# The last sum of a decode kernel: x added by TensorE, the result turned onto 128 partitions and stored as 128 short rows

## The chip, the core and the metric

The kernel runs on one NeuronCore of a Trainium2 chip (trn2). The metric is the device time of one execution in microseconds (us); three executions of the kernel before took 1304.88, 1305.26 and 1305.73 us, median 1305.26. The profile is of one further execution. In it and in the text, PE is the matrix engine (TensorE), PEld its loading of weights, DVE the vector engine, ACT the scalar engine, POOL is GpSimd, and SP the engine that issues most of the transfers. DMA engines, 16 of them, move data between the device memory and SBUF (the on-chip memory of 128 partitions); matmuls write to PSUM, a smaller memory beside PE, likewise of 128 partitions.

## The reference

One token (a vector x of 512 floats) goes through a layer norm, and then through attention over a cache of 65536 keys and an MLP, side by side. The result is the sum of both and of x itself. All is float32.

```python
xn = _layernorm(x, axis=-1)
return x + _A_ref(xn, A_k_cache, A_v_cache, A_wq, A_wo) + _B_ref(xn, B_w1, B_w2)

# _A_ref: 32 query heads, 8 key/value heads of 65536 keys x 128
q = (x @ wq).reshape(...)
scores = einsum("bhqd,bhkd->bhqk", q, k) * (Dh ** -0.5)
o = einsum("bhqk,bhkd->bhqd", softmax(scores), v)
return o.reshape(B, Sq, Hq * Dh) @ wo          # 4096 -> 512

# _B_ref
h = maximum(einsum("bsd,df->bsf", x, w1), 0)   # 512 -> 1792
return einsum("bsf,fd->bsd", h, w2)            # 1792 -> 512
```

The caches are 2 x 268 MB, the weights some 24 MB; everything is read once.

## The kernel before, in words

The kernel is written with one queue of instructions for each engine and explicit semaphores. A small class, Flow (lines 43 to 65), counts an engine's instructions: `op` issues one, after waiting for the marks that it is given, and `mark` is the engine's count so far. The helper `load` (line 150) issues one DMA and makes a semaphore for it; all loads and the one store go through its line 152, so in the profile they stand under L152 (the loads of k and v in the loop stand under L175, L297 and L299).

The work goes in four stages.

1. Start. x is loaded twice on ACT's queue: as 128 rows of 4 floats (tile xT, for the layer norm) and as 4 rows of 512 bytes at partitions 0, 32, 64 and 96 of the tile x4 (line 202; x4 is cleared before by DVE). wq is loaded on SP's queue, and q is made.
2. The loop over 8 heads x 4 parts of the cache (32 steps). SP loads 8 MB of k and 8 MB of v for each step as soon as the buffers ks and vs are free. PE makes scores (L329), DVE turns them by 32x32 blocks (L361, a stream transpose from PSUM), ACT takes the exponential (L407), PE multiplies with v (L345), DVE accumulates (L387).
3. The MLP's first half. w1 and w2 go into ks and wo into vs, when these are free. wo is cut into 32 slices of 128 x 512 floats and loaded by six DMAs of 16, 8, 4, 2, 1 and 1 slices (line 38), so that the last to land is small.
4. The end, lines 423 to 521. PE multiplies with w1 (L428), DVE takes the maximum with 0 (L435) and turns it (L269), PE and DVE put the heads' sums together (L439 to L472). Then comes the last product. `gather` (L483) accumulates 14 slices of w2 and the first 24 slices of wo, each of 512 columns with one column of weights; slice j goes to row 32 x (j mod 4) of the PSUM tile acc_z. So four matmuls stand side by side in the array, each on its own 32 of the 128 columns, and acc_z holds four partial sums of the same 512 values. DVE copies acc_z to `rows` (L498). Then acc_y takes over: its row 32c, with c from 0 to 3, holds the 128 results 128c to 128c + 127. L501 sums the four partial sums into it with a column of ones, one matmul for each c. The last eight slices of wo (j from 24 to 31) go straight to acc_y, four matmuls a slice, one for each c (L510). DVE adds x (L516), in place in x4, and SP stores 4 rows of 512 bytes (line 518). SP then waits for the store (line 521), and the engines' closing semaphores end the execution.

PE's instructions are carried out in the order in which they are written, and what sets that order at the end is the order of the slices of wo. Between the copy L498 and the store there is no other work for PE, DVE and SP.

The change lies in stage 4. The functions that it touches:

Of the kernel before, what the change touches and what calls it, by code (L numbers as in the profile page):

```python
# [15 lines left out]
P = 128  # L16
# [5 lines left out]
CT = 4  # L22
# [13 lines left out]
SLICES = R * G  # L36
# [32 lines left out]
def attention_and_mlp_kernel(  # L69
# [29 lines left out]
    te, ve, se, ge, sy = nc.tensor, nc.vector, nc.scalar, nc.gpsimd, nc.sync  # L99
# [4 lines left out]
    def place(name, *shape):  # L104
        return sb.tile([P, *shape], F32, name=name)
# [3 lines left out]
    tr = place("tr", NT * SUB, 32)  # L109
    wt = place("wt", NT * SUB, G)  # L110
    xT, xc, sq, xn = (place(n, A) for n in ("xT", "xc", "sq", "xn"))
    x4 = place("x4", P)
    sw = place("sw", SLICES)
    mine = place("mine", HKV)

# [5 lines left out]
    ident, ones = place("ident", P), place("ones", P)  # L121
# [13 lines left out]
    rows = place("rows", 512)  # L135
# [4 lines left out]
    acc_o, acc_z, acc_y, pm = (ps.tile([P, 512], F32, name=n) for n in ("acc_o", "acc_z", "acc_y", "pm"))  # L140

    names = "k_in v_in tiles scores m_out bias_out a_out w_out o_out k_free v_free q_in d_out f_out f_free"
    with tc.tile_critical():
# [4 lines left out]
        PE, DV, AC, GP = (Flow(nc, e, n) for e, n in ((te, "pe"), (ve, "dve"), (se, "act"), (ge, "pool")))  # L148

        def load(engine, name, dst, src, n=16):  # L150
            sem = nc.alloc_semaphore(name)
            engine.dma_start(dst, src).then_inc(sem, n)  # L152
            return sem, n
# [33 lines left out]
        for t in (acc_o, acc_z, pm):  # L187
# [6 lines left out]
                out=ident, in_=ident, pattern=[[-1, P]], base=0, channel_multiplier=1,  # L194
# [5 lines left out]
        x4_in = None  # L200
        se.wait_ge(*x4_free)
        x4_in = load(se, "x4_in", x4[0:P:32, :], x.rearrange("(c n) -> c n", c=CT))
# [72 lines left out]
        for i in range(SLICES):  # L275
            c = i % CT
# [3 lines left out]
                    start=(i < CT), stop=(i >= SLICES - CT),  # L280
# [41 lines left out]
        with nc.Fori(0, STEPS, engines=[ENG.PE]):  # L322
            te.wait_ge(k_in, 16).then_inc(k_in, -16)
            te.wait_ge(q_in, 1).then_inc(q_in, -1)  # L324
            for s in range(NT):
                pt = (pa, pb)[s // 2 % 2][:, s % 2, :]
                for c in range(CT):
                    at = (s * CT + c) * TW
                    i = te.matmul(pt[32 * c : 32 * c + 32, :], qcur, ks[:, at : at + TW], start=True, stop=True)  # L329
# [12 lines left out]
            n = NT * SUB // WIDE  # L342
            for i in range(n):
                c = i % CT
# [4 lines left out]
                    start=(i < CT), stop=(i >= n - CT),  # L349
# [5 lines left out]
        with nc.Fori(0, HKV, engines=[ENG.DVE]):  # L355
            for n in range(NP):
                for s in range(0, NT, 2):
                    if s == NT - 2:

                        ve.wait_ge(s_tiles, NT // 2).then_inc(k_free, 1)  # L360
                    i = ve.transpose(  # L361
                        tr[:, s * SUB : (s + 2) * SUB, :].rearrange("p b i -> p (b i)"),
                        (pa, pb)[s // 2 % 2].rearrange("p i k -> p (i k)"),
                    )._wait_ge(s_tiles, s // 2 + 1)
# [5 lines left out]
                i = ve.reduce_max(top, tr[:, :, :G].rearrange("p b g -> p g b"), axis=AX.X)  # L370
                if n:
                    ve.drain()
                    i = ve.tensor_max(m, m, mc)  # L373
# [29 lines left out]
        with nc.Fori(0, HKV, engines=[ENG.Activation]):  # L403
            for n in range(NP):
                se.wait_ge(s_bias, 1).then_inc(s_bias, -1)  # L405
                for g in range(G):
                    i = se.activation(  # L407
                        wt[:, :, g], tr[:, :, g], AF.Exp, bias=bias[:, n, g : g + 1],
                        scale=scale, accum_out=part[:, n, g : g + 1],
                    )  # L410
# [13 lines left out]
        for a in range(A):  # L424
            for c in range(CT):
# [4 lines left out]
                        start=(a == 0), stop=(a == A - 1),  # L430
# [49 lines left out]
        def gather(c, lhsT, row, marks, last=False):  # L480

            PE.op(
                lambda e: e.matmul(acc_z[32 * c : 32 * c + 1, :], lhsT, row, start=c not in begun, stop=last),  # L483
                *marks,
            )
            begun.add(c)

        for j in range(FB):
            gather(j % CT, hT[:, j : j + 1], t2[:, j * D : (j + 1) * D], [hT_in, w2_in])

        for j in range(SLICES):
            row = vs[:, j * D : (j + 1) * D]
            lhsT = sw[:, j : j + 1]
            if j < DIRECT:
                gather(j % CT, lhsT, row, [sw_in, wo_in[j]], last=(j >= DIRECT - CT))
                if j == DIRECT - 1:

                    DV.op(lambda e: e.tensor_copy(rows, acc_z), PE.mark)  # L498
                    for c in range(CT):
                        PE.op(  # L500
                            lambda e: e.matmul(  # L501
                                acc_y[32 * c : 32 * c + 1, :P], ones[:, 0:1], rows[:, c * P : (c + 1) * P],
                                start=True, stop=False,
                            ),
                            DV.mark,
                        )
            else:
                for c in range(CT):
                    PE.op(
                        lambda e: e.matmul(  # L510
                            acc_y[32 * c : 32 * c + 1, :P], lhsT, row[:, c * P : (c + 1) * P],
                            start=False, stop=(j == SLICES - 1),
                        ),
                        sw_in, wo_in[j],
                    )
        DV.op(lambda e: e.tensor_add(x4, acc_y[:, :P], x4), PE.mark, x4_in)  # L516
        sy.wait_ge(*DV.mark)
        done = load(sy, "y_out", out.rearrange("(c n) -> c n", c=CT), x4[0:P:32, :])

    with tc.tile_critical():  # L520
        sy.wait_ge(*done)
# [29 lines left out]
```

## Time and profile before

| | |
|---|---|
| median of three executions | 1305.26 us (1304.88 to 1305.73) |
| the profiled execution's own time | 1305.38 us |
| its span, from first to last instruction | 1303.3 us |
| read from device memory | 560.99 MB, 430 GB/s over the span |
| PE busy | 662.4 us (51%) |
| DVE busy | 268.9 us (21%) |
| ACT busy | 75.9 us (6%) |
| granted PE clock, mean | 0.734 of full |
| granted PE clock, 1293 us to 1302 us | 1.00 |
| last copy of acc_z (L498) | starts at 1296.95 us |
| last matmul (L510) | ends at 1300.08 us |
| add of x (L516) | 1300.10 us, 0.29 us long |
| issue of the store on SP | 1300.42 us, 0.67 us long |

Shares are of the span. A group line of the profile has the line in the kernel, the engine, the operation, output <- inputs, shapes (partitions x elements) and count; then busy us and mean ns of one; then the engine's idle time before it and what ended it. A timeline line has start and length in us first. Starts count from the span's start. A float32 matmul leaves two records, since PE goes over it twice. Matmuls are pipelined: the length of a record has the way through the array in it, so the pace is read from the distance of starts and not from the length of one.

### The profile page before, as it was taken

What the parts mean: (1) busy time and instruction counts of PE and PEld (TensorE: products, weight loads), DVE (VectorE), ACT (ScalarE), POOL (GpSimd) and SP (SyncE); (2) the same over time, 40 slices, a digit from 0 to 9 for tenths busy, and PEclk for the clock granted to TensorE, in tenths of its full rate; (3) what the DMA queues carried; (4) which work ended last, traced back from release to release, by engine and by line L of the source; (5) the groups of instructions that cost most, each with busy time, mean ns of one, the idle gap of its engine ahead of it and who ended that gap; (6) DMA issues with size and microseconds to landing.
All of it is one profiled execution on the core that took longest, in us unless ns stands there. A gap on an engine that the chain in (4) does not pass through costs nothing. (4 is left out here: it accounts for less than half of the span.)

```text
span 1303.3 us, 10616 instructions
## 1 busy us (share of the span) xinstructions
PE 662.4 (51%) x4562; PEld 243.2 (19%) x4562; DVE 268.9 (21%) x395; ACT 75.9 (6%) x292; POOL 5.4 (0%) x22
## 2 busy tenths in 40 slices
PE   4355446445445535445545535544544644553657
PEld 2121112112112112111211111221111212111123
DVE  2221122221122222012222112222112222211222
ACT  0000000000000000000000000000000000000000
POOL 0000000000000000000000000000000000000000
PEclk9677687777677677677778677767767666767768
DMA  9999999999999999999999999999999999999998
GB/s 418 419 445 422 447 422 447 420 447 422 440 428 430 438 422 445 424 445 424 445 422 447 422 447 420 443 426 436 432 426 443 424 443 424 445 424 445 422 429 346
DMA packets 10821, 561.06 MB, mean 430 GB/s; under 512 B 1336, under 2 KB 1344, under 8 KB 1728
## 3 DMA queue, kind: packets, MB, share of 16 engines
q1 hardware_dynamic: 10664, 560.99, 99.5%
q8 instruction: 3, 0.05, 0.0%
q10 hardware_dynamic: 152, 0.00, 0.0%
q14 instruction: 2, 0.02, 0.0%
HBM read 560.99 MB, written 0.00 MB: 430 GB/s over the span
## 5 line engine op out<-in xcount | busy, mean ns | idle before, releaser
L345 PE MATMUL acc_o<-vs,wt 128*16 128x512 f32 x2048 | 292.0, 734 | 180.1 <-PEq L341 180.1
L329 PE MATMUL pa<-ks,qcur 128*32 128x512 f32 x1024 | 183.6, 814 | 328.9 <-PEq L324 328.9
L361 DVE STREAM_TRANSPOSE tr<-pa 128x1024 f32<-128x1024 f32 x64 | 80.0, 1250 | 421.4 <-PE pa L329 421.4
L329 PE MATMUL pb<-ks,qcur 128*32 128x512 f32 x1024 | 144.0, 653 | 0.0
L329 PEld LDWEIGHTS pa<-ks,qcur 128*32 128x32 f32 x1024 | 64.3, 133 | 416.2 <-issue 403.7
L345 PEld LDWEIGHTS acc_o<-vs,wt 128*16 128x16 f32 x2048 | 68.9, 113 | 376.4 <-issue 376.4
L407 ACT ACTIVATE wt<-tr,bias 128x128 f32<-128x128 f32 x128 | 64.3, 511 | 1085.3 <-ACTq L405 1085.3
L387 DVE SCALAR_TENSOR_TENSOR acc<-acc,alpha,acc_o 128x512 f32<-128x512 f32 x24 | 17.9, 747 | 352.5 <-PE acc_o L345 352.5
L361 DVE STREAM_TRANSPOSE tr<-pb 128x1024 f32<-128x1024 f32 x64 | 80.0, 1250 | 45.5 <-PE pb L329 45.5
L329 PEld LDWEIGHTS pb<-ks,qcur 128*32 128x32 f32 x1024 | 66.2, 129 | 78.3 <-issue 58.4
L334 PE MATMUL pm<-ident,m 128*4 128x128 f32 x32 | 10.0, 313 | 87.0 <-DVE m L373 66.6
L385 DVE COPY acc<-acc_o 128x512 f32<-128x512 f32 x8 | 5.5, 692 | 118.9 <-PE acc_o L345 118.9
L335 PE MATMUL pm<-dg,ones 4*128 4x4 f32 x64 | 15.0, 302 | 21.4 <-DVE dg L377 21.4
L370 DVE TENSOR_REDUCE mc<-tr 128x4 f32<-128x512 f32 x24 | 24.1, 1006 | 1.8
L334 PEld LDWEIGHTS pm<-ident,m 128*4 128x4 f32 x32 | 2.6, 81 | 116.0 <-DVE m L373 88.4
L407 ACT ACTIVATION_READ_ACCUMULATOR wt<-tr,bias 128x1 f32 x128 | 23.9, 187 | 0.0
L335 PEld LDWEIGHTS pm<-dg,ones 4*128 4x128 f32 x64 | 12.2, 236 | 28.8 <-DVE dg L377 28.8
L336 PE MATMUL pm<-dg,rowg 4*128 4x1 f32 x64 | 14.3, 290 | 0.0
L336 PEld LDWEIGHTS pm<-dg,rowg 4*128 4x128 f32 x64 | 13.0, 249 | 0.0
L278 PE MATMUL pa<-vs,tr 128*8 128x512 f32 x64 | 9.9, 769 | 6.1 <-DMA vs<-wq 4.8
L375 DVE TENSOR_REDUCE mg<-pm 4x1 f32<-4x128 f32 x32 | 8.9, 279 | 13.0 <-PE pm L334 13.0
L378 DVE COPY bias<-pm 128x5 f32<-128x5 f32 x32 | 5.2, 163 | 27.8 <-PE pm L336 27.8
(90 smaller groups left out, 116.6 us busy)
## 6 DMA issues: line engine op xcount, KB each, us to landing
vs<-wq SPq DMA_DIRECT2D x1, 7168.0 KB, 21.4
ks<-w SPq DMA_DIRECT2D x2, 3584.0 KB, 22.1
vs<-wo SPq DMA_DIRECT2D x1, 4096.0 KB, 16.4
vs<-wo SPq DMA_DIRECT2D x1, 2048.0 KB, 20.9
vs<-wq SPq DMA_DIRECT2D x1, 1024.0 KB, 4.9
vs<-wo SPq DMA_DIRECT2D x1, 1024.0 KB, 22.9
ks<-k SPq DMA_DIRECT2D x32, 29.2
vs<-v SPq DMA_DIRECT2D x32, 29.3
```

The source lines that it names most:

```text
L278: lambda e: e.matmul(pr[32 * c : 32 * c + HKV, :], xs[:, i, :], vs[:, i * 512 : (i + 1) * 512], start=(i < CT), stop=(i >= SLICES - CT),),
L329: i = te.matmul(pt[32 * c : 32 * c + 32, :], qcur, ks[:, at : at + TW], start=True, stop=True)
L334: te.transpose(pm[:G, :P], m, ident)._wait_ge(s_dve, 3).then_inc(s_max, 1)
L335: te.matmul(pm[:, P : P + G], ones[:G, :], dg[:, :G], start=True, stop=True)._wait_ge(s_dve, 4)
L336: te.matmul(pm[:, P + G : P + G + 1], rowg, dg[:, G : G + 1], start=True, stop=True).then_inc(s_max, 1)
L345: mm = te.matmul(acc_o[32 * c : 32 * c + WIDE * G, :], wt[:, i * WIDE : (i + 1) * WIDE, :].rearrange("p b g -> p (b g)"), vs[:, i * 512 : ...
L361: i = ve.transpose(tr[:, s * SUB : (s + 2) * SUB, :].rearrange("p b i -> p (b i)"), (pa, pb)[s // 2 % 2].rearrange("p i k -> p (i k)"),)._ ...
L370: i = ve.reduce_max(top, tr[:, :, :G].rearrange("p b g -> p g b"), axis=AX.X)
L375: ve.reduce_max(mg, pm[:G, :P], axis=AX.X)._wait_ge(s_max, 1)
L385: ve.tensor_copy(flat, acc_o)
L387: ve.scalar_tensor_tensor(flat, flat, alpha[:, n : n + 1], acc_o, op0=ALU.mult, op1=ALU.add)
L407: i = se.activation(wt[:, :, g], tr[:, :, g], AF.Exp, bias=bias[:, n, g : g + 1], scale=scale, accum_out=part[:, n, g : g + 1],)
```

## The change

Four things are changed, all in stage 4.

- The places in acc_y. Row 32c still holds results 128c to 128c + 127, but result 4i + j of them now lies in column 32j + i. To that end the moving operand of every matmul into acc_y is read in another order: `cut` takes the 128 columns of c, and goes over i (32 values, a step of 4 floats) inside j (4 values, a step of 1 float). `places4` writes them in order.
- x. Four more matmuls, behind those of L501: the row 32c of x4, one partition, with a single one as weight, is added to row 32c of acc_y. The vector engine's add is gone, and the wait on the load of x4 stands on PE now.
- The turn. In place of the add, DVE transposes acc_y by 32x32 blocks into a new tile yt (128 partitions x 32 x 4 floats, 512 bytes a partition). Row 32c of block j becomes column 0 of the transposed block, and the output is written with a step of 4 floats, so that the four floats `yt[p, 0, :]` of partition p are the results 4p to 4p + 3.
- The store. One DMA of 128 rows of 16 bytes from yt, in place of 4 rows of 512 bytes from x4. Both are issued by SP through line 152.

```diff
-    x4 = place("x4", P)
+    x4, yt = place("x4", P), place("yt", 32, 4)
...
+        def cut(row, c):
+
+            return row[:, c * P : (c + 1) * P].rearrange("p (i j) -> p j i", j=4)
+
+        def places4(c):
+            return acc_y[32 * c : 32 * c + 1, :P].rearrange("p (j i) -> p j i", j=4)
+
...
                         PE.op(
                             lambda e: e.matmul(
-                                acc_y[32 * c : 32 * c + 1, :P], ones[:, 0:1], rows[:, c * P : (c + 1) * P],
-                                start=True, stop=False,
+                                places4(c), ones[:, 0:1], cut(rows, c), start=True, stop=False,
                             ),
                             DV.mark,
+                        )
+                    for c in range(CT):
+                        own = slice(32 * c, 32 * c + 1)
+                        PE.op(
+                            lambda e: e.matmul(
+                                places4(c), ones[own, 0:1], cut(x4[own], 0), start=False, stop=False,
+                            ),
+                            x4_in,
                         )
             else:
                 for c in range(CT):
                     PE.op(
                         lambda e: e.matmul(
-                            acc_y[32 * c : 32 * c + 1, :P], lhsT, row[:, c * P : (c + 1) * P],
-                            start=False, stop=(j == SLICES - 1),
+                            places4(c), lhsT, cut(row, c), start=False, stop=(j == SLICES - 1),
                         ),
                         sw_in, wo_in[j],
                     )
-        DV.op(lambda e: e.tensor_add(x4, acc_y[:, :P], x4), PE.mark, x4_in)
+
+        DV.op(lambda e: e.transpose(yt.rearrange("p i j -> p j i"), acc_y[:, :P]), PE.mark)
         sy.wait_ge(*DV.mark)
-        done = load(sy, "y_out", out.rearrange("(c n) -> c n", c=CT), x4[0:P:32, :])
+        done = load(sy, "y_out", out.rearrange("(p j) -> p j", j=4), yt[:, 0, :])
```

## The prediction

> **What bounds the kernel now.** I read the page's slices first, then the timeline of the last 35 us, then groups by form, then the issues of the load helper (L152) and the semaphore instructions behind the store.
>
> The page's head, its DMA row (busy tenths of the DMA engines in 40 slices) and its HBM row:
>
> ```profile
> span 1303.3 us, 10616 instructions
> ...
> DMA  9999999999999999999999999999999999999998
> ...
> HBM read 560.99 MB, written 0.00 MB: 430 GB/s over the span
> ```
>
> The DMA engines are full in every slice but the last: the kernel streams 561 MB, and no engine's work in the loops sets the time. The change touches nothing before the last slices, so it can win or lose only in the tail, where DMA has run dry. The timeline of that tail (start us, length us, engine, line, operation, operands, count, idle before it):
>
> ```profile
> 1283.14 3.62 PE L461 MATMUL pb<-oT,tr 128*128 128x32 f32 x16 [0.28 <-DVE oT L458]
> 1286.69 4.52 PE L483 MATMUL acc_z<-ks,hT 128*1 128x512 f32 x26
> ...
> 1296.95 0.69 DVE L498 COPY rows<-acc_z 128x512 f32<-128x512 f32 x1 [9.08 <-PE acc_z L483]
> 1297.69 0.10 PEld L501 LDWEIGHTS acc_y<-rows,ones 128*1 128x1 f32 x8 [1.84 <-DVE rows L498]
> 1297.69 0.40 PE L501 MATMUL acc_y<-rows,ones 128*1 128x128 f32 x8 [0.91 <-DVE rows L498]
> 1297.80 1.52 PEld L510 LDWEIGHTS acc_y<-vs,sw 128*1 128x1 f32 x56
> 1297.91 2.05 PE L510 MATMUL acc_y<-vs,sw 128*1 128x128 f32 x64
> 1299.56 0.10 PEld L510 LDWEIGHTS acc_y<-vs,sw 128*1 128x1 f32 x8 [0.23 <-DMA vs<-wo]
> 1300.10 0.29 DVE L516 TENSOR_TENSOR x<-acc_y,x 128x128 f32<-128x128 f32 x1 [2.46 <-PE acc_y L510]
> 1300.42 0.67 SPq L152 DMA_DIRECT2D y<-x  x1
> ```
>
> From 1296.95 on this is one chain: copy, 4 matmuls of L501, 32 of L510, add, store. Each f32 matmul is two records. Four matmuls, one for each 32-row block of acc_y, run side by side; I call them a group. A group's pitch is 0.22 us (L501 starts at 1297.69, the next group at 1297.91; the loads say the same, 56 records or 7 groups in 1.52). Eight groups of L510 and one of L501 lie here. The last waited for its slice of wo: its natural start is 1297.91 + 7 x 0.218 = 1299.44, its real one 1299.56. So the slack that DMA gives PE is 0.12 us. The last matmul ends at 1300.08.
>
> **The change, part by part.** The sum is made against the profiled execution: 1305.38 us, of which 1303.3 is span and 2.08 lies around it. The runs' median, 1305.26, is 0.12 below it.
>
> *The extra group (x by PE).* Four more matmuls behind L501: one more group, 0.22. Its wait on x4's load hides behind everything (issued at 1.4 us, landed by 10.1). With reads at today's rate, 0.12 of the 0.22 is taken out of the wait for wo: +0.10. Its rows are one partition each, so the array is used in another shape and then goes back. The row for a change of shape is L461 (128 columns of weights) to L483 (one): the last of L461 ends at 1286.76, L483 starts at 1286.69, so nothing is emptied; but L483 starts 0.33 after the last L461 start, against L461's pitch of 0.22, so 0.11 is lost. Bounds for two switches: 0, and 2 x (0.27 duration - 0.11 pitch of one record) = 0.33, if the array empties each time. I take 0.1, near the row. The Trainium skill, TensorEngine Tiling (Array Packing), Key Properties, says that a change of tiling mode drains the engine; the trace at L461 to L483 shows no drain, and by that rule the term would be 0.33 and the sum 0.2 higher.
>
> *The strided reads.* This is the term that decides. All ten groups (L501, x, eight of L510) now read their moving operand with a step of 4 floats, 16 bytes, since cut() puts j outside i. PE reads one element in 0.109/128 = 0.85 ns today (two records per 0.218 us, four streams side by side). No matmul of this trace reads with such a step, so I bound by the vector engine's rows:
>
> ```profile
> L400 DVE TENSOR_REDUCE fin<-masked 128x128 f32<-128x512 f32 x1 | 1.1, 1062 | 0.0
> ...
> L394 DVE TENSOR_TENSOR masked<-acc,selb 128x512 f32<-128x512 f32 x1 | 0.7, 683 | 0.0
> L472 DVE TENSOR_REDUCE sw<-tr 128x32 f32<-128x256 f32 x1 | 0.6, 611 | 0.0
> L465 DVE TENSOR_TENSOR tr<-pb,mine 128x256 f32<-128x256 f32 x1 | 0.4, 425 | 3.7 <-PE pb L461 3.7
> ```
>
> L394 and L465 read in order: (683 - 425)/256 = 1.01 ns an element and 167 ns fixed. L472 reads SBUF with exactly a step of 16 bytes (h inside g), L400 with 512: (611 - 167)/256 = 1.73 and (1062 - 167)/512 = 1.75 ns. So a stepped float costs 1.73 ns there. If PE's reads are held to the same 1.73 ns, a group goes from 0.218 to 0.218 x 1.73/0.85 = 0.44. Lower bound: no cost. Upper bound beside 0.44: PE's four streams share what one has, 4 x 0.218 = 0.87. I take 0.44, the nearest row by step, type and memory. Before: last matmul ends at 1297.69 + 8 x 0.218 + 0.31 tail = 1299.74 for the eighth group, then the DMA wait, 1300.08. After: 1297.69 + 10 x 0.44 + 0.31 = 1302.40, and the wait for wo is long over. Difference +2.3, extra group included; DMA no longer covers any of it.
>
> *The vector instruction.* An add of 128 elements (291 ns) becomes one transpose of 128 x 128 from PSUM. The profile's row for one is L361: 1250 ns for 1024 columns; at 1.04 ns a column that leaves 183 fixed, so 316 ns for 128. It writes with a step of 16 bytes; if writes pay as reads do, 183 + 128 x 1.73 = 404. So +0.03 to +0.11; I take +0.06. Nothing covers it: PE ended before, SP waits behind.
>
> *The store.* The issues of L152 at the start and the end, and what follows on SP (duration min/median/max in ns; start range):
>
> ```profile
> L152 ACTq DMA_DIRECT2D xT<-x x1: 413/413/413, 0.9 to 0.9; - x1
> L152 ACTq DMA_DIRECT2D x<-x x1: 1075/1075/1075, 1.4 to 1.4; - x1
> ...
> L152 SPq DMA_DIRECT2D y<-x x1: 667/667/667, 1300.4 to 1300.4; - x1
> ...
> L143 SPq EVENT_SEMAPHORE  x3: 17/28/28, 1301.5 to 1301.8; - x3
> ```
>
> The two 4-row transfers hold their queue 1.10 us until the next instruction (y: 1300.42 to 1301.52; x4 the same on ACT); a 128-row one holds SP 0.46 (wq, 0.96 to 1.41). So SP is free 0.64 sooner. But SP then waits for the landing: the trace's semaphore record has the store's last increment at 1302.11, 1.69 after the issue, and SP's wait for it ends at 1302.17, just in the cadence of the instructions before it. So the landing starts to bind as soon as SP is earlier. What it becomes: xT, the one load of 128 rows of 16 bytes, moved its first packet 1.05 after issue (y 1.27); the first packets of the 16 engines spread over some 0.25 (wq's queue); eight packets of 7 ns each, some 0.05 to 0.1; from y's semaphore packets to the landing 0.33. Together 1.05 + 0.25 + 0.08 + 0.33 = 1.71 against 1.69: nothing gained or lost. Bounds: -0.3 if the engines start together and the landing follows at once; +2.3 if each engine's eight rows go one after another at 0.33 each (7 x 0.33). I take 0, since xT is the nearest row.
>
> *Sum.* +2.3 (PE) + 0.1 (shape) + 0.06 (DVE) + 0 (store) = +2.46 on 1305.38: 1307.8 by the profiled execution, 1307.7 by the median.
>
> **Rivals.**
> - *PE reads with a step for free* (chance 0.22). For: PE already takes 0.85 ns for a float, and its port is not the vector engine's. Against: 0.85 is still half of 1.73. Then +0.10 + 0.1 + 0.06 = +0.26: 1305.5. The Trainium skill, SBUF — State Buffer, Specifications (TRN2), wants two hits per 16-byte line for full bandwidth; no run here shows that for PE, and by it this case loses to mine.
> - *Faster* (0.07). Reads free, and the store's engines start together, so that the landing comes at 1.39: +0.26 - 0.3 = 0 to -0.3 with a shape change at no cost: 1305.1. The point from which it decides: the landing has to come more than 0.26 us earlier than 1.69. For: SP is released 0.64 sooner. Against: xT landed 4.3 after its issue (beside other loads), not 1.4.
> - *The small rows are slow to land* (0.06): up to +2.3 on top of my sum, half of it as a middle: 1308.9; on free reads 1306.7. For: nothing in this trace writes 16-byte rows. Against: xT's packets took 7 ns each. The Trainium skill, DMA: Bandwidth & Descriptors, Specifications, says that under 512 bytes the engine reads, modifies and writes; no run here shows it.
> - *The four streams share one read rate* (0.05): ten groups of 0.87, +6.7: 1312.0. Against: today four streams keep the pitch that one stream's records have.
>
> **How the numbers follow.** My case has 0.60. Its own range is 1306.9 (1.45 ns an element, no cost for the shape) to 1308.5 (shape 0.33, DVE 0.11, a store later by 0.3). Over all cases 1305.1 to 1308.5 leaves out about half of the faster case, most of the slow landing and the shared streams, under 0.2 together. 0.2% is 2.6 us, about what a measurement of this kernel can tell from no change: above 1307.87 is slower. My forecast lies just inside, so 0.40 of my case goes over (0.24), with most of the last two rivals: slower 0.33. Below 1302.6 nothing worked out here reaches: faster 0.01. Same 0.66.
>
> **What would show it.** The groups of the last eight slices of wo at a pitch of 0.44 instead of 0.22, with no wait for wo on the last: right; at 0.22: the free reads. The transpose's duration, 316 to 404 ns. The store's issue at some 0.41 instead of 0.67, and the next instruction on SP 0.46 behind its start. The landing 1.7 after the issue. It is wrong if PE's pitch stays, if the gap around the x group is longer than 0.33, or if the store lands later than 2 us after its issue.

## The result and the profile after

| | before | after |
|---|---|---|
| median of the executions (22 of each, side by side) | 1305.32 us (1304.88 to 1305.73) | 1307.32 us (1307.05 to 1308.00) |
| ratio, 95% interval | | 1.0016 (1.0009 to 1.0023) |
| the profiled execution's own time | 1305.38 us | 1307.57 us |
| its span | 1303.3 us | 1305.5 us |

The change makes the kernel slower by 2.0 us, 0.16%: clear of zero, and inside the 0.2% that the prediction took as its bound.

The page after, its head, the DMA row (busy tenths) and the HBM row:

```profile
span 1305.5 us, 10631 instructions
...
DMA  9999999999999999999999999999999999999997
...
HBM read 560.99 MB, written 0.00 MB: 430 GB/s over the span
```

The stream is what it was; the last slice of the DMA row is emptier by a tenth, in line with a tail without transfers that is longer by 2 us. The tail in the timeline of after (start us, length us, engine, line, operation, operands, count, idle before; L508 is now the sum of rows, L516 the group of x, L524 the slices of wo, L530 the turn):

```profile
1296.69 0.69 DVE L505 COPY rows<-acc_z 128x512 f32<-128x512 f32 x1 [11.35 <-PE acc_z L483]
...
1297.43 0.63 PE L508 MATMUL acc_y<-rows,ones 128*1 128x128 f32 x8 [0.89 <-DVE rows L505]
1298.00 0.10 PEld L516 LDWEIGHTS acc_y<-x,ones 1*1 1x1 f32 x8 [0.46 <-issue]
1298.00 0.63 PE L516 MATMUL acc_y<-x,ones 1*1 1x128 f32 x8
1298.55 3.28 PEld L524 LDWEIGHTS acc_y<-vs,sw 128*1 128x1 f32 x64 [0.46 <-issue]
1298.56 3.81 PE L524 MATMUL acc_y<-vs,sw 128*1 128x128 f32 x64
1302.51 0.41 DVE L530 STREAM_TRANSPOSE yt<-acc_y 128x128 f32<-128x128 f32 x1 [5.13 <-PE acc_y L524]
1302.94 0.35 SPq L152 DMA_DIRECT2D y<-yt  x1
```

What the reader is to see: the 64 records of wo take 3.81 us where they took 2.05 with the wait for the last slice in it. No weight load waits for DMA any more (before, the last eight waited 0.23). The groups of L508, L516 and L524 begin at 1297.43, 1298.00 and 1298.56, 0.56 apart, of which 0.45 is a group and the rest a gap.

The store's issue and the semaphore instructions of SP behind it (duration min/median/max in ns; range of starts):

```profile
L152 SPq DMA_DIRECT2D y<-yt x1: 347/347/347, 1302.9 to 1302.9; - x1
```
```profile
L143 SPq EVENT_SEMAPHORE  x3: 17/28/28, 1303.7 to 1304.0; - x3
```

From the issue to SP's next instruction 0.76 us pass (1302.94 to 1303.70), before it was 1.10; from the issue to the end of the span 2.56, before 2.90.

The two profiles add up. From the first matmul into acc_y to the end of the last (as DVE is released), PE takes 5.05 us instead of 2.39: +2.66. The turn takes 408 ns where the add took 291: +0.12. The store gives 0.34 back. The copy of acc_z happens to start 0.26 earlier in the profile of after: -0.26. The sum is +2.18; the spans differ by 2.19.

### The profile page after: what moved, and what is told of

Its sections match the earlier page's. It is cut to its first block, busy times and chain, and to the rows that moved or that the text cites. A ratio compares the mean times of both kernels' runs of the same rounds, so it can differ in the third digit from the quotient of the medians.

```text
span 1305.5 us, 10631 instructions
## 1 busy us (share of the span) xinstructions
PE 673.0 (52%) x4570; PEld 248.1 (19%) x4570; DVE 269.1 (21%) x395; ACT 75.9 (6%) x292; POOL 5.3 (0%) x22
## 5 line engine op out<-in xcount | busy, mean ns | idle before, releaser
L345 PE MATMUL acc_o<-vs,wt 128*16 128x512 f32 x2048 | 295.5, 742 | 176.3 <-PEq L341 176.3
L329 PE MATMUL pb<-ks,qcur 128*32 128x512 f32 x1024 | 147.1, 664 | 0.0
L329 PEld LDWEIGHTS pb<-ks,qcur 128*32 128x32 f32 x1024 | 69.4, 131 | 77.9 <-issue 58.5
```

The lines of the kernel that those rows point to most:

```text
L345: mm = te.matmul(acc_o[32 * c : 32 * c + WIDE * G, :], wt[:, i * WIDE : (i + 1) * WIDE, :].rearrange("p b g -> p (b g)"), vs[:, i * 512 : ...
```

## The experiments

The theory: the reads with a step of 16 bytes double PE's time for every group into acc_y, and all else is small. The main rival: the extra group with its change of shape, or the turn and the store, make the loss. Where a kernel "reads in order", the host lays out the columns of wo and, in the same way, w2 in the order in which acc_y wants them (`order` is that permutation), which needs no arithmetic and no step in the reads; the result stays the same.

Times are medians, of 10 or 11 executions of each kernel and 19 or 26 of the kernel before.

| kernel | time, us | before beside it, us | ratio (95% interval) |
|---|---|---|---|
| stepped reads alone | 1306.78 | 1305.23 | 1.0012 (1.0002 to 1.0022) |
| after, reads in order | 1305.23 | 1305.23 | 1.0000 (0.9991 to 1.0010) |
| x on PE alone | 1305.50 | 1305.22 | 1.0001 (0.9992 to 1.0011) |
| turn and store alone | 1305.16 | 1305.22 | 0.9999 (0.9990 to 1.0009) |
| x early, reads in order | 1305.08 | 1305.22 | 0.9999 (0.9989 to 1.0008) |

The other kernels ran once each; what they are for is read from their profiles, not from their times.

### Stepped reads alone

The kernel before, with the reads of after; DVE's add reads PSUM back in the right order.

```diff
-  acc_y[32 * c : 32 * c + 1, :P], lhsT, row[:, c * P : (c + 1) * P],
+  places4(c), lhsT, cut(row, c),
...
-  DV.op(lambda e: e.tensor_add(x4, acc_y[:, :P], x4), PE.mark, x4_in)
+  x4_out = x4.rearrange("p (i j) -> p i j", j=4)
+  DV.op(lambda e: e.tensor_add(x4_out, acc_y[:, :P].rearrange("p (j i) -> p i j", j=4), x4_out), PE.mark, x4_in)
```

> The kernel before with one thing changed: every matmul into acc_y reads its moving operand with a step of 16 bytes; DVE's add reads PSUM back in the right order, x stays with DVE, the store stays 4 rows. Theory (the stepped reads make the loss): the groups' pitch is 0.45 us instead of 0.22, nine groups end some 1.9 to 2.1 later (9 x 0.235 less the 0.12 of slack to the last slice of wo), time 1307.2 to 1307.4. Rival (the extra group of x with its change of shape, or the turn, makes the loss, and a stepped read only lengthens a matmul's way through the array): pitch 0.22, time 1305.3 to 1305.6.

The timeline of this kernel (as above):

```profile
1297.19 0.63 PE L507 MATMUL acc_y<-rows,ones 128*1 128x128 f32 x8 [0.89 <-DVE rows L504]
1297.40 3.53 PEld L516 LDWEIGHTS acc_y<-vs,sw 128*1 128x1 f32 x64
1297.63 3.83 PE L516 MATMUL acc_y<-vs,sw 128*1 128x128 f32 x64
1301.60 0.29 DVE L524 TENSOR_TENSOR x<-acc_y,x 128x128 f32<-128x128 f32 x1 [4.46 <-PE acc_y L516]
```

Eight groups of loads in 3.53 us: the pitch is 0.44 to 0.45; the trace's starts give 0.227 for each pass over a group where before it is 0.109. PE takes 4.38 us for nine groups; the nine of before take 2.26 without the wait for wo. That is +2.12 for the step alone. The time rises by 1.55, less than I had expected (1.9 to 2.1): the slack to wo is larger than the 0.12 that I read from the profile of before (below). The rival is out as the main cause: nothing of x, the turn or the new store is in this kernel.

One thing more is in this trace. DVE's add reads PSUM here with a step of 32 floats, 128 bytes, and takes 293 ns where it took 291 in order. So not every stepped read costs.

### After, with its reads in order

```diff
+  order = np.arange(D).reshape(CT, 32, 4).transpose(0, 2, 1).reshape(D)
...
-  "wo": np.asarray(A_wo).reshape(HKV, G, DH, D).transpose(0, 2, 1, 3),
+  "wo": np.asarray(A_wo).reshape(HKV, G, DH, D).transpose(0, 2, 1, 3)[..., order],
...
-  places4(c), lhsT, cut(row, c), start=False, stop=(j == SLICES - 1),
+  places4(c), lhsT, row[:, c * P : (c + 1) * P], start=False, stop=(j == SLICES - 1),
```

> The kernel after with its reads put in order: the columns of wo and w2 are laid out on the host in the order in which acc_y wants them, so only the four matmuls of x read with a step. x on PE, the turn and the 128-row store stay. Theory: the groups of rows and of wo go back to a pitch of 0.22, the x group keeps 0.45 and two gaps of 0.12 around it, PE ends 0.3 later than before, the transpose costs 0.12 more than the add, the store gives 0.34 back: time within 0.3 of before, 1305.1 to 1305.6, some 2 below after. Rival (x's group, its change of shape and the turn make the loss): it stays at 1307.0 to 1307.5.

```profile
1297.27 0.40 PE L508 MATMUL acc_y<-rows,ones 128*1 128x128 f32 x8 [0.89 <-DVE rows L505]
...
1297.60 0.63 PE L516 MATMUL acc_y<-x,ones 1*1 1x128 f32 x8
1298.16 1.63 PEld L524 LDWEIGHTS acc_y<-vs,sw 128*1 128x1 f32 x64 [0.46 <-issue]
1298.16 1.93 PE L524 MATMUL acc_y<-vs,sw 128*1 128x128 f32 x64
```

The slices of wo are back at 1.93 us, x's group alone keeps the long form (0.63 with its step), and the whole loss is gone: 1305.23 on both sides. So without the step the rest of the change, x on PE, turn and store, comes out at nothing that the times show, and with it the change costs 2.0. Alone the step cost 1.55: there it had the slack to wo all to itself, while in the change the group of x and its change of shape (PE takes 2.94 us here for 2.26, +0.68) have used that slack up already.

### A step of 8 bytes, a step of 32

The first experiment with `j=2` and `j=8` in `cut` and `places4`.

> As the stepped reads alone, but with a step of 2 floats (8 bytes). If what costs is that each read opens a new stretch of 16 bytes, two reads in a row fall into one stretch here and the pitch of a group stays 0.22, time as before. If any step costs, the pitch is 0.45 and the time 1307.3. If the cost goes with the bytes passed over, the pitch lies half way, 0.33, and the time near 1306.2.

> As the stepped reads alone, but with a step of 8 floats (32 bytes). If each read of a new 16-byte stretch costs the same, the pitch is 0.45 again and the time 1307.3. If the cost goes with the bytes passed over, the pitch is near 0.9 and the time near 1311.

The group of wo's slices in the three kernels, steps of 8, 16 and 32 bytes in this order (count | busy us, mean ns of one record | idle before and what ended it); in the kernel before the mean is 272:

```profile
L516 PE MATMUL acc_y<-vs,sw 128*1 128x128 f32 x64 | 2.4, 274 | 0.2 <-DMA vs<-wo 0.2
```
```profile
L516 PE MATMUL acc_y<-vs,sw 128*1 128x128 f32 x64 | 3.8, 405 | 0.0
```
```profile
L516 PE MATMUL acc_y<-vs,sw 128*1 128x128 f32 x64 | 3.9, 413 | 0.0
```

The pitch of a pass over a group is 0.113, 0.227 and 0.233 us (0.109 in order); for one float 0.88, 1.77 and 1.82 ns. So it is not the step as such, and the price does not grow with the bytes passed over. Nor does it follow the number of rows in the access pattern (2, 4 and 8 here). It is there where no two reads in a row fall into the same 16 bytes, and is then a factor of two. Any other limit between 8 and 16 bytes would fit these steps as well; a step of 12 was not run. The Trainium skill, SBUF — State Buffer, Specifications (TRN2), states lines of 16 bytes that need two hits each for full bandwidth; the trace agrees, with 0.113 at two hits and 0.227 at one on PE.

### x on PE alone, and x over the full column

The first is the kernel before with x's four matmuls, read in order, and DVE copying. The second is the kernel after with a column of the identity as weights, so that x's matmuls use all 128 rows of the array, like their neighbours.

```diff
-  places4(c), ones[own, 0:1], cut(x4[own], 0), start=False, stop=False,
+  places4(c), ident[:, 32 * c : 32 * c + 1], cut(x4, 0), start=False, stop=False,
```

> The kernel before with x on PE alone: four matmuls of one row behind those of the copy, read in order; DVE copies acc_y into x4, 4 rows are stored. Theory: one group of 0.22 and two gaps of 0.12 at the change of shape, less the 0.12 of slack to wo: PE ends 0.3 later, time 1305.5 to 1305.7. Rival (the x group is what makes the loss of 2): 1307.

> The kernel after with x's matmuls over all 128 rows of the array, a column of the identity as weights (x4 is zero outside its four rows). If the gaps of 0.12 in front of and behind x's group come from the change of shape, they go: the groups of rows, x and wo run at one pitch of 0.45 and PE's part from the first of these to the last matmul's end falls from 5.05 to 4.8. If they come from the wait on x's load or from the step, they stay.

The time of the first, 1305.50, can't be told from before. Its groups do tell: the sum of rows starts at 1297.29, x at 1297.62, wo at 1297.94, 0.33 apart, a group of 0.22 and a gap of 0.11 each time. In the second kernel:

```profile
1297.74 0.63 PE L508 MATMUL acc_y<-rows,ones 128*1 128x128 f32 x8 [0.91 <-DVE rows L505]
...
1298.17 0.65 PE L515 MATMUL acc_y<-x,ident 128*1 128x128 f32 x8
...
1298.63 3.83 PE L523 MATMUL acc_y<-vs,sw 128*1 128x128 f32 x64
```

Starts 0.43 and 0.46 apart, where after has 0.56: the gaps are gone, with the wait on x's load and the step still there. PE takes 4.84 us for its part instead of 5.05. So the two changes of shape cost 0.21 together. (This kernel's single time, 1307.68, is above after's median; its copy of acc_z stood 0.3 later than in the profile of after.) The Trainium skill, TensorEngine Tiling (Array Packing), Key Properties, has a change of tiling mode drain the engine; a price of 0.11 for each change agrees with it in kind, and is below the 0.16 that I had as the bound for an emptied array.

### The turn and the store alone; the turn written in order

The first of these is the kernel with reads in order and without x on PE; DVE adds x to the turned result, `yt[:, 0, :] + xT`.

> The turn and the 128-row store alone: reads in order by the host layout, no matmul of x; x is added by DVE to the turned result (128 x 4, from xT), one more short instruction. Theory: PE as before; transpose +0.12, the small add with its wait +0.2, store -0.34: 1305.2 to 1305.4, the same as before. Rival (the small rows are slow to land, or the transpose waits): 1306 or more.

Its time is that of before, 1305.16 against 1305.22: the turn (0.41 for the add's 0.29), a second short DVE instruction (0.16 and a gap) and the end of the store, shorter by 0.34, cancel.

```diff
-  DV.op(lambda e: e.transpose(yt.rearrange("p i j -> p j i"), acc_y[:, :P]), PE.mark)
+  DV.op(lambda e: e.transpose(yt.rearrange("p j i -> p (j i)"), acc_y[:, :P]), PE.mark)
```

Here yt is placed as 4 x 32 floats, and `yt[:, 0, 0:4]` is stored: as many rows and bytes, but not the result.

> The kernel after with the transposed blocks written in order instead of with a step of 16 bytes; what is stored is then not the result, but as many rows and bytes. If the 0.09 of the turn above the 316 ns that the long transposes of the loop give comes from the stepped write, the transpose takes 316 ns; if 128 columns simply cost more than their share of 1024, it stays at 408. The rest as after.

```profile
1302.26 0.32 DVE L530 STREAM_TRANSPOSE yt<-acc_y 128x128 f32<-128x128 f32 x1 [5.13 <-PE acc_y L524]
```

317 ns by the trace, 408 with the step: the step in the write costs 0.09, that is 0.7 ns for each of the 128 floats, as much as the step cost DVE's reads in the prediction's rows (1.73 against 1.01).

### x early

Reads in order, and x's four matmuls ahead of the sum of rows instead of behind it, where PE waits for the copy of acc_z; with the identity's columns, so that the shape stays.

```diff
   DV.op(lambda e: e.tensor_copy(rows, acc_z), PE.mark)
+  for c in range(CT):
+      PE.op(lambda e: e.matmul(places4(c), ident[:, 32 * c : 32 * c + 1], cut(x4, 0), start=True, stop=False), x4_in)
   for c in range(CT):
       ...
-      start=True, stop=False,
+      start=False, stop=False,
```

> In-order reads as above (host layout of wo and w2), and x's four matmuls moved ahead of the copy of acc_z, where PE waits for DVE, with a column of the identity as weights so that all 128 rows of the array are used and its shape does not change. The turn and the 128-row store stay. Theory: x costs nothing, PE ends as before (1300.1), the transpose costs 0.12, the store gives 0.34 back: 0.2 under before, 1305.0 to 1305.2. Rival (x on PE costs wherever it stands, or the turn and the store cost more than they give): 1305.3 or more.

```profile
1296.28 0.63 PE L508 MATMUL acc_y<-x,ident 128*1 128x128 f32 x8
...
1296.61 0.69 DVE L505 COPY rows<-acc_z 128x512 f32<-128x512 f32 x1 [11.41 <-PE acc_z L483]
...
1299.57 0.11 PEld L523 LDWEIGHTS acc_y<-vs,sw 128*1 128x1 f32 x8 [0.52 <-DMA vs<-wo]
1299.58 0.40 PE L523 MATMUL acc_y<-vs,sw 128*1 128x128 f32 x8 [0.23 <-DMA vs<-wo]
1300.12 0.41 DVE L529 STREAM_TRANSPOSE yt<-acc_y 128x128 f32<-128x128 f32 x1 [2.82 <-PE acc_y L523]
```

x is through (1296.91) before the sum of rows can begin (1297.36), and PE waits for the last slice of wo again. From that slice's landing (by the trace's semaphore record) to the end of the span it takes 3.58 us, before 3.80: 0.22 less, which is the store's 0.34 less the turn's 0.12. The medians differ by 0.14 in the same direction, but their interval does not exclude zero: that this kernel beats the kernel before is shown in the tail's profile and not by the clock.

### The store by rows

The kernel with x early, but the 2 KB leave from neighbouring partitions, in fewer rows. What is stored is then not the result. The edit for 16 rows, with 8 and 4 made the same way:

```diff
-  done = load(sy, "y_out", out.rearrange("(p j) -> p j", j=4), yt[:, 0, :])
+  done = load(sy, "y_out", out.rearrange("(p f) -> p f", f=32), yt.rearrange("p i j -> p (i j)")[0:16, 0:32])
```

> The kernel with x early, but the 2 KB are stored as 16 rows of 128 bytes (from the first 16 partitions, so not the result). If what shortens the store is that all 16 DMA engines take part, SP's hold stays at 0.76 and the landing near 1.4 after the issue, or a little sooner. If it is the number of rows as such, both move back toward those of 4 rows, 1.10 and 1.69.

> The same with 8 rows of 256 bytes. If it needs all 16 engines, this behaves as 4 rows: SP held 1.10, landing 1.67 or so. If it goes with the number of rows, it lies between 4 and 16 rows.

> The kernel with x early, stored as 4 rows of 512 bytes from four neighbouring partitions (so not the result), where the kernel before takes partitions 0, 32, 64 and 96. 8 rows held SP 0.79. If few rows are what holds SP, this one is held 1.10 and lands at 1.67, as before. If it is the step of 32 partitions in the source, it is held some 0.8 and lands at 1.2 to 1.3.

From the starts in the traces and their semaphore record, us after the start of the store's issue:

| rows x bytes | partitions | SP's next instruction | first packet | landed | end of SP's instruction that waits for it |
|---|---|---|---|---|---|
| 4 x 512 (before) | every 32nd | 1.10 | 1.27 | 1.69 | 1.78 |
| 4 x 512 | neighbours | 0.77 | 0.78 | 1.20 | 1.43 |
| 8 x 256 | neighbours | 0.79 | 0.80 | 1.21 | 1.45 |
| 16 x 128 | neighbours | 0.78 | 0.86 | 1.35 | 1.43 |
| 128 x 16 (after) | all | 0.76 | 0.84 | 1.41 | 1.43 |

The issue itself in the second kernel of the table, from the load helper's line:

```profile
L152 SPq DMA_DIRECT2D y<-yt x1: 352/352/352, 1300.7 to 1300.7; - x1
```

It is 667 ns in the kernel before, for as many rows of as many bytes. Both expectations for 8 rows failed, and the last run answers them: what held SP was neither few rows nor few DMA engines. What is left is the source of the old store, which takes every 32nd partition. It lies in another tile too (x4, not yt), and a store of neighbouring partitions of x4 was not run. The load of x4, which writes to every 32nd partition, points the same way: its issue takes 1075 ns, that of xT's load, with 128 rows, 413. Short rows are no help: 128 of 16 bytes land 0.21 later than 4 of 512. That is hidden but for some 0.02, since SP reaches its wait no sooner than 1.39 in any of the last four kernels. So what the change gains at the store, 0.34, is SP's hold, 0.76 in place of 1.10.

## Why the prediction was right, and where its sizes were off

It named the loss, its place and its cause, and the time, 1307.7 against 1307.32, lies 0.4 from it, well inside the range. That the number came so close is in part luck: PE and the turn were taken 0.33 too cheap, the slack and the store 0.70 too dear, and these errors cancel in part. Point by point:

- *Strided reads.* Right, and nearly in size. Borrowed from the vector engine's rows was 1.73 ns a float, PE takes 1.77; the pitch is 0.454 instead of 0.44, over ten groups 0.14 more. Nothing tied PE to the vector engine's rate, and no run explains why the two come so close (PE about twice its own 0.85 in order, DVE 1.7 times its own 1.01): this part is luck. The rival of free reads falls with the first two experiments, and that of four streams sharing one rate (a pitch of 0.87) with the same numbers.
- *The extra group.* Its wait on x4's load costs nothing, as said. The shape was mis-sized: 0.21 for two changes, taken as 0.1. The nearest row had shown 0.11 for one change, and I took that for two; the end of 0.33 was too high. I had read no drain from that row, because the end of one record lies behind the start of the next; the loss shows in the starts.
- *The vector instruction.* 408 ns, the upper end given (404); I had taken half of the step's price.
- *The store.* Off: 0 was taken, -0.34 measured, just beyond the lower bound of -0.3. Two terms were wrong. The start of the engines was taken from xT and wq, 1.05 us to the first packet and 0.25 of spread, both measured at the kernel's start beside other loads; here it is 0.84, and all 128 packets start within 0.19. And SP's hold of 0.46 was read from a load with another load behind it; after the store SP's next instruction comes 0.41 after the issue has ended (before 0.43), which the row for wq does not have. What lies in that 0.41 stays open.
- *The rival of small rows slow to land.* It did not come: 1.41 us. The Trainium skill, DMA: Bandwidth & Descriptors, Specifications, has transfers under 512 bytes read, modify and write. The bytes read from device memory are the same to the byte in both traces (560,992,256), so no such read shows; the rows do land 0.21 later than 4 of 512 bytes.
- *The slack to wo.* 0.12 was right for the profile of before and not typical. From the start of the copy to the landing of the last slice of wo it is 2.57 us there, and 2.81 to 3.18 in the thirteen other profiles, median 2.93. So PE can usually be 0.48 late for nothing. With this, the terms give the time that was measured: PE's part without waits 5.05 - 2.26 = +2.79, less 0.48, turn +0.12, store -0.34: +2.09, and the medians differ by 2.00. The surplus of my sum, 2.46, is mostly these two, the slack and the store, against a shape and a step taken too cheap.
- *Two slips in the working.* The end of before without its wait is nine pitches behind 1297.69, not eight: 1299.96 and not 1299.74; the sum does not use it. And the upper end of the case's own range, with the terms named there, comes to 1308.3 and not 1308.5.

## What to carry to other kernels

Before a layout is turned by the access pattern of a matmul's moving operand, look at the step: float32 read with a step of 16 or 32 bytes halved PE's rate, with 8 bytes it cost 4%. A permutation of a weight's columns in the host's layout did the same for nothing, and an addend can go into PSUM first, while PE waits anyway. DVE's add read PSUM with a step at no price; whether its transpose would too, so that the order could be made there, was not run. A slack that is read from one profile is one draw; where a term rests on it, look at how the two events that bound it move against each other.

## What was not expected of the hardware

- A store of 4 rows of 512 bytes from every 32nd partition held SP 1.10 us and landed after 1.69; from four neighbouring partitions of another tile it was 0.77 and 1.20.
- A change from matmuls over 128 rows of the array to one row, and the change back, cost 0.11 us each, at full clock.
- The vector engine's transpose pays for a stepped write: 408 ns against 317 for 128 x 128. Its add paid nothing for a stepped read of PSUM: 293 ns against 291.
